# A new issue order for a gated long-convolution and mixer kernel: second-level table zeroed before the last level's index is made

## The chip, the cores and the metric

The kernel runs on one core of a Trainium2 chip. The core has TensorE (PE, matmuls), VectorE (DVE), ScalarE (ACT), GpSimd (POOL), and SyncE (SP), which here issues DMAs only. The metric is device microseconds of one execution. Before the change the median of three runs is 243.41 us (242.63 to 243.48).

## The reference: what is computed

```
x = A_q                                        # 2048 x 512, bf16
k_shift = sum over 4 taps of shifted A_k * A_shift_k
kv      = k_shift * A_v
y       = causal convolution of kv with A_ssm_k (length 2048, by FFT) + kv * A_ssm_D
h       = x + layernorm(x) * y
# mixer on layernorm(h)
g   = gelu(layernorm(.) @ w1); its four column quarters shifted by 1, -1, 2, -2 rows
x1  = . + g_shifted @ w2
out = h + x1 + gelu(layernorm(x1) @ w3) @ w4
```

## The kernel before

All data stays in SBUF. The program first records about 920 operations with what each reads and writes, and then emits them in a hand-over order, the text `ISSUE`: a list of operation numbers. Where an operation may run on either of two engines, a letter behind its number says which (`V` DVE, `A` ACT, `G` POOL). Each engine executes its own operations strictly in the order of that list and waits, where it must, for what an operation reads. So a late input holds back everything behind it on that engine. The microseconds given to `add` and its helpers are the cost model from which the list was searched; they are not executed.

The work runs in these steps. The names are those used below.

- **Loads.** SP issues `k0..k3`, `v0..v3` (L240, L244) and `h0..h3` (L249), each 512 KB, and eight transfers of q (L430), each 256 KB.
- **k side.** k is transposed on PE and copied (`kT`, L171 on ACT or L173 on DVE: all plain copies out of PSUM show one of these two lines). Four taps are PE matmuls (`psh`, L477). DVE multiplies by v (`kvq`, L481), for four row quarters and two column halves. SP moves each result into another layout by two SBUF-to-SBUF transfers, the k rows (`Rk`, L488).
- **h side.** POOL adds A_ssm_D into column 0 of h (L563, once for h0 and h2, once for h1 and h3); PE transposes (`pt`, L502), ACT or DVE copies (`Rh`).
- **First level.** PE matmuls `pah` (from `Rh`) and `pak` (from `Rk`, L518), 16 each, copied out as `Th` and `Tk` by ACT or DVE.
- **Second level.** 32 PE groups `pc` (L542 to L544) against the block-diagonal table `Wc`; each is copied out (`xt`). `Wc` is zeroed by 12 POOL memsets (L411) and then filled by four DMAs (L414).
- **Product.** Per pair of groups DVE does a complex product (`pr`, L674, and `Yr`, `Yi`, L688 and L690).
- **Inverse.** 16 PE groups `pg` (L744), copied out as `Gs`. When all 16 are done the PSUM pools are exchanged and the last level begins.
- **Last level.** 8 PE groups `py` (L797) against `Wf`, whose angles come from an index made by POOL (iota, L344) and two DVE passes each on two halves (`uf`, L351 and L354), and two ACT sines (L358). The result is scaled by the row's normalisation (`y`, L805 on ACT, L807 on DVE), gated with q (`hs`, L812), its statistics are taken (L620, L621), a Newton chain of ten small DVE operations (`rh`, L601 to L605 and others) gives the scale, and ACT or DVE normalises (`hn`, L840, L843). This is done in four blocks of four row tiles, b0 to b3.
- **Mixer.** For b0 and b1 PE transposes `hn`, for b2 and b3 SP does it by DMA transposes (L900). Then come the matmuls with w1 (L868, gelu on ACT, L872), w2 (L945, `x1` on DVE), w3 (L868) and w4 (L1014), and the stores.

q is normalised beside this: statistics (`bst`, L624), means, and a centring of each of 16 tiles (`qc`, L634 on ACT, L636 on DVE). ACT loads the gelu table (L423) once, after its last sine.

Of the kernel before, what the change touches and what calls it, by code (L numbers as in the profile page):

```python
# [42 lines left out]
19 89 91 4 87 78 1 0 2 30 92 31 22 5 20 33 88 23 7 6 8 25 12 32 24 34V 42 35 41 40 43 48 93 10 26 90 28 29 95 15  # L43
14 21 36 38 45 46 39 98 44 49 50 51 99V 100V 96A 104 9 54 139 47 18 105V 52V 55V 3 97A 56 37 17 53 57 11 101
102A 103A 107 106A 13 142 140 84 75 111 83 60 108 27 141V 143A 74 166 16 68 167A 112 144 113 115 116 114 160 76
80 230 228 229 231 63 240 241 253V 61 161A 79 158 254V 65 147 110 159A 145 148A 77 62 152 146V 119 153A 109 255A
151 120 156 157A 127 118 162 222 220 66 64 221 58 198 117 128 223 122 123 236 121 194 252A 124 237 246V 163A 131
59 199A 164 149 195A 247V 176 178 132 81 165A 172 177A 82 173A 179V 190 180 170 181A 191V 171A 245V 135 244A 168
192 224 227 136 67 182 174 193V 169A 183A 154 273 155V 175A 225 226 238 239 250V 275 69 188 189A 72 186 248V 184
187A 185A 70 272 71 73 281 283 282V 276 284A 285 138 277A 86 130 249V 251V 278 279A 280 295 196 296A 85 293 129  # L50
288 197A 290 287 286 125 307 234 294A 297 137 235 289A 291A 305 292 308A 300 302 134 233 232 126 306A 260 242
150 301A 298 133 210 216V 261 204 303A 211V 208 205A 200 209A 212 299 324 262 214 304 263 264 201A 243 274 213A
265 314 206 215V 202 315A 312 266 319 207A 203A 313A 317 327 309 320A 267 310 318A 311 332 328A 325 330 268 333A
217V 337 326A 269 259V 316 331A 270 218V 321 322 323 329 339 338A 381 334 335 340A 344 342 336 349 271 345A 341
# [74 lines left out]
def kernel(  # L133
# [927 lines left out]
```

## Time and profile before

| | us |
|---|---|
| profiled execution, its own time | 243.34 |
| its span | 241.5 |
| PE busy | 224.7 (93%) |
| DVE busy | 161.0 (67%) |
| ACT busy | 153.1 (63%) |
| POOL busy | 15.4 (6%) |

The profile gives times from the start of the span; 1.84 us of the execution lie outside it. PE's busy time holds matmuls on zeros (L440, L880) that only keep it running, so its 93% doesn't say that PE is the bound everywhere. The granted TensorE clock is full in all 40 slices. Rows of the timeline read: start, duration, engine, line, operation, and in brackets the idle time before it and what ended that. Rows with several pieces are merged.

### The profile page before, as it was taken

What the parts mean: (1) busy time and instruction counts of PE and PEld (TensorE: products, weight loads), DVE (VectorE), ACT (ScalarE), POOL (GpSimd) and SP (SyncE); (2) the same over time, 40 slices, a digit from 0 to 9 for tenths busy, and PEclk for the clock granted to TensorE, in tenths of its full rate; (3) what the DMA queues carried; (4) which work ended last, traced back from release to release, by engine and by line L of the source; (5) the groups of instructions that cost most, each with busy time, mean ns of one, the idle gap of its engine ahead of it and who ended that gap; (6) DMA issues with size and microseconds to landing.
All of it is one profiled execution on the core that took longest, in us unless ns stands there. A gap on an engine that the chain in (4) does not pass through costs nothing.

```text
span 241.5 us, 5031 instructions
## 1 busy us (share of the span) xinstructions
PE 224.7 (93%) x2069; PEld 147.6 (61%) x2069; DVE 161.0 (67%) x380; ACT 153.1 (63%) x205; POOL 15.4 (6%) x30
## 2 busy tenths in 40 slices
PE   8899987998899977999969999999999999999994
PEld 7899987897799864574434544444444444444454
DVE  6954999999999997999998899910440044004421
ACT  5788769999979998889657399763036204630000
POOL 2359300000000000000000000000000000000000
PEclk9999999999999999999999999999999999999999
DMA  6998876740000099100640025320002012001111
GB/s 218 391 374 203 168 187 213 174 91 3 0 3 0 20 343 390 39 0 0 88 84 5 1 53 99 61 52 3 10 22 54 0 24 65 0 0 42 46 43 45
DMA packets 22182, 21.82 MB, mean 90 GB/s; under 512 B 11916, under 2 KB 18704, under 8 KB 22160
## 3 DMA queue, kind: packets, MB, share of 16 engines
q1 hardware_dynamic: 21904, 21.37, 32.7%
q8 instruction: 16, 0.26, 0.5%
q10 hardware_dynamic: 256, 0.14, 0.2%
q14 instruction: 6, 0.05, 0.1%
HBM read 13.11 MB, written 2.10 MB: 63 GB/s over the span
## 4 chain that ended last, share of the span: by engine, by line
PE 51%; DVE 25%; DMA 12%; ACT 6%; issue 2%; SPq 1%; DVEq 0%; ACTq 0%
PE pw L868 23%; PE p L1014 20%; DVE kin L674 6%; DMA kin<-in_A_v_dram 5%; PE p L945 4%; DVE bst L620 4%; DVE ab L173 4%; ACT s L171 3%; DMA q_sb<-in_A_q_dram 3%; ACT ab L171 3%; DMA kin<-in_A_k_dram 2%; DVE ab L812 2%; DMA act<-ab 2%; DVE kin L688 1%; DVE bst L624 1%
## 5 line engine op out<-in xcount | busy, mean ns | idle before, releaser
L868 PE MATMUL pw<-act,wts 128*128 128x512 bf16 x288 | 64.0, 379 | 2.5 <-DMA act<-ab 1.9
L872 ACT ACTIVATE ab<-pw 128x512 bf16<-128x512 f32 x56 | 33.0, 596 | 38.4 <-PE pw L868 27.3
L1019 DVE TENSOR_TENSOR wts<-p,wts 128x1024 bf16<-128x1024 f32 (+2 forms) x10 | 10.1, 1012 | 62.0 <-PE p L1014 62.0
L868 PEld LDWEIGHTS <-wts 128*128 128x128 bf16 x288 | 28.0, 98 | 36.3 <-DMA act<-ab 2.4
L1014 PE MATMUL p<-wts,ab 128*128 128x512 bf16 (+1 forms) x238 | 48.9, 366 | 0.0
L1014 PEld LDWEIGHTS <-ab 128*128 128x128 bf16 x238 | 23.3, 98 | 25.3
L542 PE MATMUL pc<-ab,Wc 128*128 128x256 bf16 x128 | 30.7, 282 | 1.4 <-DVE ab L173 1.1
L171 ACT CAST s<-pc 128x1024 bf16<-128x1024 f32 x31 | 29.6, 1044 | 1.4 <-DVE kin L674 1.3
L544 PE MATMUL pc<-ab,Wc 128*128 128x128 bf16 x128 | 29.0, 227 | 0.0
L543 PE MATMUL pc<-ab,Wc 128*128 128x128 bf16 x128 | 28.0, 219 | 0.0
L543 PEld LDWEIGHTS <-Wc 128*128 128x128 bf16 x128 | 19.4, 151 | 1.4 <-issue 1.4
L674 DVE TENSOR_TENSOR kin<-s 128x2048 bf16<-128x2048 bf16 x16 | 19.4, 1221 | 0.6
L542 PEld LDWEIGHTS <-Wc 128*128 128x128 bf16 x128 | 19.4, 151 | 0.3
L544 PEld LDWEIGHTS <-Wc 128*128 128x128 bf16 x128 | 18.2, 142 | 0.0
L477 PE MATMUL psh<-ab 128*128 128x128 bf16 x256 | 15.6, 219 | 0.4 <-DVE kvq L481 0.4
L171 ACT CAST ab<-pah 128x1024 bf16<-128x1024 f32 x13 | 12.8, 1023 | 4.8 <-PE pah L518 4.8
L477 PEld LDWEIGHTS <-ab 128*128 128x128 bf16 x256 | 14.4, 98 | 0.9 <-issue 0.4
L945 PE MATMUL p<-wts,act 128*128 128x512 bf16 x64 | 15.0, 379 | 0.0
L481 DVE TENSOR_TENSOR kvq<-psh,kin 128x1024 bf16<-128x1024 f32 x8 | 9.7, 1218 | 4.8 <-DMA kin<-in_A_v_dram 4.8
L171 ACT CAST ab<-pak 128x1024 bf16<-128x1024 f32 x13 | 12.5, 1061 | 0.0
L951 DVE SCALAR_TENSOR_TENSOR s<-ab,rho,p 128x512 bf16<-128x512 bf16 x16 | 11.5, 739 | 1.2 <-PE p L945 1.1
L1000 DVE SCALAR_TENSOR_TENSOR wts<-s,mq,ab 128x512 f32<-128x512 bf16 x16 | 11.2, 749 | 0.2
(139 smaller groups left out, 316.3 us busy)
## 6 DMA issues: line engine op xcount, KB each, us to landing
wts<-in_B_w_dram SPq DMA_DIRECT2D x2, 1792.0 KB, 11.1
kin<-in_A_k_dram SPq DMA_DIRECT2D x4, 512.0 KB, 5.8
ab<-in_A_ssm_k_dram SPq DMA_DIRECT2D x4, 512.0 KB, 8.6
kin<-in_A_v_dram SPq DMA_DIRECT2D x4, 512.0 KB, 13.6
q_sb<-in_A_q_dram SPq DMA_DIRECT2D x8, 256.0 KB, 6.1
kin<-kvq SPq DMA_DIRECT2D x16, 128.0 KB, 5.1
out_dram<-wts SPq DMA_DIRECT2D x14, 128.0 KB, 2.3
Wc<-ab SPq DMA_DIRECT2D x4, 384.0 KB, 5.3
```

The source lines that it names most:

```text
L171: A.copy(o, src)
L477: T_.matmul(pv[:, g, i, :], lhsT=row(g, 4 * qr + i - j), rhs=dg()[:, 2 * g + cc, j, :], start=(j == 0), stop=(j == 3))
L542: T_.matmul(pv[:, kk], lhsT=W[0], rhs=T[:, :, 2 * k1:2 * k1 + 2, :], start=True, stop=False)
L543: T_.matmul(pv[:, kk, :, 0, :], lhsT=W[1], rhs=T[:, :, 2 * k1 + 1, :], start=False, stop=False)
L544: T_.matmul(pv[:, kk, :, 1, :], lhsT=W[2], rhs=T[:, :, 2 * k1, :], start=False, stop=True)
L674: v(1.13, lambda: V.tensor_tensor(out=prs(), in0=xs(0).unsqueeze(1).to_broadcast([P, 2, 2, 512]), in1=xs(1).unsqueeze(2).to_broadcast([P, ...
L868: T_.matmul(ps[:], lhsT=wt(w)[:, k, m * P:(m + 1) * P], rhs=xT()[:, k, 4 * b * P:(4 * b + 4) * P], start=(k == 0), stop=(k == DC - 1))
L872: add({"A": 0.49}, lambda: A.activation(dst(), X[pkey][:], ACT.Gelu_apprx_tanh), r + [pkey, "gelu"], [key])
L945: T_.matmul(ps[:, i, :], lhsT=gT()[:, m, t + i + 2 + off[m], :], rhs=wt("w2")[:, m, :], start=(m == 0), stop=(m == 3))
L951: v(0.66, lambda t=t, i=i, key=key: V.scalar_tensor_tensor(out=qn()[:, t + i, :], in0=hn()[:, t + i, :], scalar=rho[:, t + i:t + i + 1], i ...
L1000: v(0.66, lambda j=j, i=i, t=t + i: V.scalar_tensor_tensor(out=ofb()[:, j, i], in0=qn()[:, t, :], scalar=mq[:, t:t + 1], in1=hs()[:, t, :] ...
L1014: T_.matmul(ps[:, i, x0:x1], lhsT=g2(b % 2)[:, m, s0:s0 + P], rhs=wt("w4")[:, m, x0:x1], start=(m == 0), stop=(m == FC - 1))
```

## The change

**Zeroing first.** POOL's queue, after the small gate operation, was: iota and hand-over for `uf`, the h addition, the 12 memsets with the second h addition after two of them. The 12 memsets now wait only for the gate, and the `uf` iotas wait for the memsets; the operation `gt2` that ordered the two goes. The POOL order is now: 3 memsets, h addition (h0, h2), 8 memsets, h addition (h1, h3), 1 memset, then for each half of `uf` an iota and the first of its two passes. Those two first passes have moved from DVE to POOL by their letter.

**k rows.** The transfers may be issued from SP or from ACT's queue, by a letter `S` or `A`.

**Scaling.** The two scalings of a `py` group become one operation with two instructions, on one engine.

**Cost model.** Some of its figures change (0.6 to 0.615, 0.08 to 0.14 and so on); these aren't executed.

**Orders.** `ISSUE` is replaced as a whole. In it all sixteen k rows have the letter `S`.

The order of SP, first part, before:

```
k3 k0 k2 k1 h2 h0 v0 h3 h1 v1 v2 q q v3 | Rk1 x2, q q, Rk0 x2, Rk2 x2, Rk3 x2 | q q, Wc x4 | second half's Rk, with q q among them
```

and after:

```
k2 k1 k0 k3 h0 v1 h2 v2 v0 h3 v3 h1 q q q q | Rk0 x2, Rk2 x2, Rk1 x2, Rk3 x2 | Wc Wc q Wc Wc q | second half's Rk | q q
```

ACT, from its last `kT` to the first `Tk`, before and after:

```
Wf Rh Wf Th7 gelu-table Th4 Th3 Rh Th0 qc Th2 qc Th5 Th15 Th13 Th6 | Tk4 ...
Th1 Th5 Th4 Rh10 Th3 Rh11 Th2 Wf Th0 Th10 Th13 | Tk2 ...
```

From there to ACT's last `Gs`, before: 13 Tk, 4 Th, 31 xt, 10 Gs, 1 qc. After: 12 Tk, 4 Th, 29 xt, 13 Gs, 2 qc, 1 Wf, the gelu table.

DVE, from its last `kT` to the first `Tk`, before and after:

```
uf x4, kvq0 Rh kvq1 kvq2, bst x4, 2 mq, 2 qc, Rh, kvq3, bst x3, kvq1', bst, mq, kvq0', mq, 2 qc, kvq2' | Tk5 ...
kvq1 kvq2 Rh Rh kvq3 Th6 kvq0, bst x4, 2 mq, 3 qc, uf, qc, bst x2, kvq0', bst, kvq2', Th7 | Tk1 ...
```

From there to DVE's last `Gs`, before: 3 Tk, 3 Th, 1 xt, 6 Gs, 1 kvq, 8 bst, 6 qc. After: 4 Tk, 2 Th, 3 xt, 3 Gs, 2 kvq, 9 bst, 3 qc, 1 uf. The 32 product operations and four copies of Wf are in both. After its last `Gs` DVE does 1 qc, the new one 5 qc and the end of q's Newton chain.

PE, after the four `kT` transposes, before: `psh0, pt, pt, psh1, pah7, psh2, pah4, pah3, pt, pt, pah0, psh3, pah2 ...`; after: `psh1, psh2, pt, pt, psh3, pah1, pah6, psh0, pah4, pah5, pt, pah3, pt, pah2, psh0', psh2', pah0, pah10, pah7, pah13, pak1, pak2 ...`.

Last level on DVE, before: one `y` half, hs0, 2 bst, hs1, 2 bst, then b0's Newton chain, within which hs2, hs3 and the statistics of b1 stand. After: one whole `y`, hs0, hs1, hs2, hs3 and all eight statistics of b0 and b1, with the Newton chains of b0 and b1 alternating at their end; b3 then goes ahead of b2. `hn`: 8 on ACT and 8 on DVE before, 10 and 6 after. On PE the order is, before: w1 for b0 and b1, two w2 pairs, w1 for b2, a w2 pair, w1 for b3; after: w1 for b0 and b1, two w2 pairs, w1 for b3, w1 for b2. SP's DMA transposes go xT 8, 11, 10, 9, 15, 14, 12, 13 before and 14, 12, 13, 15, 8, 11, 10, 9 after.

```diff
-            i = int(word.rstrip("AVG"))
+            i = int(word.rstrip("AVGS"))
...
-    for hf in range(2):
-        iota(1.05, lambda hf=hf: uf(hf), [[1, 16], [32, 64]], 16 * hf, ("uf", hf), ["C", "gate"])
-        phase(0.68, lambda hf=hf: uf(hf), k1F, offF, ("uf", hf), ["C"])
-    gt2 = cst.tile([P, 2], I32)
-    add({"G": 0.2}, lambda: G.tensor_copy(gt2[:], ...
     for q in range(4):
         for a in range(3):
             add({"G": 0.95}, lambda q=q, a=a: G.memset(
-                X["Wc"][:, q, a].rearrange("p d n k -> p (d n k)").bitcast(U32), 0), ["W", "gate2"], [("wz", q, a)])
+                X["Wc"][:, q, a].rearrange("p d n k -> p (d n k)").bitcast(U32), 0), ["W", "gate"], [("wz", q, a)])
...
+    for hf in range(2):
+        iota(1.05, lambda hf=hf: uf(hf), [[1, 16], [32, 64]], 16 * hf, ("uf", hf),
+             ["C"] + [("wz", q, a) for q in range(4) for a in range(3)])
+        phase(0.68, lambda hf=hf: uf(hf), k1F, offF, ("uf", hf), ["C"])
...
-            dma(0.63, lambda g=g: nc.sync.dma_start(
+            add({"S": 0.63, "A": 0.5}, lambda e, g=g: (nc.scalar if e == "A" else nc.sync).dma_start(
...
-        for i in range(2):
-            def scaled(e, i=i, t=2 * u + i):
+        def scaled(e):
+            for i in range(2):
+                t = 2 * u + i
...
-            add({"A": 0.53, "V": 0.6}, scaled, ["W", key, ("rq", 0)], [("y", u % 4, i)])
+        add({"A": 1.18, "V": 1.22}, scaled, ["W", key, ("rq", 0)], [("y", u % 4)])
```

More of the change, by code (lines that the diff above doesn't have):

```diff
@@ L402 @@
     hold()
-    for hf in range(2):
-        iota(1.05, lambda hf=hf: uf(hf), [[1, 16], [32, 64]], 16 * hf, ("uf", hf), ["C", "gate"])
-        phase(0.68, lambda hf=hf: uf(hf), k1F, offF, ("uf", hf), ["C"])
-    gt2 = cst.tile([P, 2], I32)
-    add({"G": 0.2}, lambda: G.tensor_copy(gt2[:], X["kin"][:, 20480:24576].rearrange(
-        "p (a x) -> p a x", a=2)[:, :, 0:2].bitcast(I32).rearrange("p a x -> p (a x)")), [("uf", 0), ("uf", 1), "C"], ["gate2"])
     for q in range(4):
@@ L588, in turned @@
                     V.tensor_scalar(o, x, -1.0, None, op0=MUL)
[L590 removed]
+            add({"V": 0.45, "A": 0.95}, turned, [("Wf", 0, hf)], [("Wf", 1, hf, c), ("kvq", 0), ("kvq", 1)], lock=True)
     mvq = cst.tile([P, NT, 2], F32)
@@ L636, in centre @@
                 V.tensor_scalar(X["q_sb"][:, t, :], X["q_sb"][:, t, :], mq[:, t:t + 1], None, op0=ADD)
-        add({"A": 0.71, "V": 0.325}, centre, [("mq", t // 4), ("bst", t)], [("qc", t)])
+        add({"A": 0.69, "V": 0.27}, centre, [("mq", t // 4), ("bst", t)], [("qc", t)])
     def rsqrt_q():
@@ L1001 @@
                     out=ofb()[:, j, i], in0=qn()[:, t, :], scalar=mq[:, t:t + 1], in1=hs()[:, t, :], op0=SUB, op1=ADD),
-                  ["W", "HH"] + [("y", k, l) for k in range(4) for l in range(2)] + [("x1", t + i), ("hs", t // 2)],
+                  ["W", "HH"] + [("y", k) for k in range(4)] + [("x1", t + i), ("hs", t // 2)],
                   [("of", j, i)])
```

84 lines of the change are left out of this document (41 added, 43 removed), and 7 rows, old and new, of the table ISSUE.

## The prediction

> **What bounds the kernel now.** I first cut the span into stretches, to see which engine is full where. After the time range, the columns are its length, the busy time (and instructions) of PE, weight loads, DVE, ACT and POOL, the granted clock, the DMA share and GB/s.
>
> ```profile
> 0.00:36.40 36.40, 33.36 (x557) 31.47 (x558) 27.26 (x61) 26.48 (x32) 15.38 (x30) 1.00 0.86 257
> 36.40:93.00 56.60, 49.91 (x716) 46.94 (x715) 55.48 (x81) 54.92 (x61) 0.00 (x0) 1.00 0.37 105
> 93.00:109.00 16.00, 14.19 (x163) 9.21 (x164) 14.14 (x51) 13.38 (x22) 0.00 (x0) 1.00 0.27 106
> 109.00:122.70 13.70, 11.56 (x64) 5.40 (x63) 13.22 (x53) 10.21 (x16) 0.00 (x0) 1.00 0.36 49
> 122.70:241.50 118.80, 115.73 (x570) 54.61 (x570) 50.86 (x139) 48.07 (x79) 0.00 (x0) 1.00 0.17 35
> ```
>
> From 36.4 to 93.0 us DVE idles 1.12 us and ACT 1.68: both are the bound, and only these gaps could be won. From 122.7 PE is full. Before 36.4, DVE and ACT have time to spare, 9.1 and 9.9 us. So the question is what work is left when the full stretch begins, and how the last level hands over to the matmuls. The chain of work that ended last names that hand-over (first line), and the timeline has its steps:
>
> ```profile
> 118.45 4.22 DMA act<-ab
> ...
> 94.28 0.69 ACT L805 ACTIVATE wts<-py,rq 128x512 bf16<-128x512 f32 x1 [0.64 <-PE py L797]
> 95.00 0.75 DVE L807 TENSOR_SCALAR wts<-py,rq 128x512 bf16<-128x512 f32 x1 [1.62 <-ACT wts L805]
> 95.78 0.69 DVE L812 TENSOR_TENSOR ab<-wts,q_sb 128x1024 bf16<-128x1024 bf16 x1
> 104.06 0.16 DVE L827 SCALAR_TENSOR_TENSOR nb<-mvh,rh 128x4 f32<-128x4 f32 x1
> 108.99 1.02 PE L868 MATMUL pw<-act,wts 128*128 128x512 bf16 x4 [0.34 <-ACT act L171]
> 117.22 3.62 PE L945 MATMUL p<-wts,act 128*128 128x512 bf16 x16
> 122.71 3.63 PE L868 MATMUL pw<-act,wts 128*128 128x512 bf16 x16 [1.88 <-DMA act<-ab]
> ```
>
> The last copies before the pool exchange end at 93.0 (the bound of the second stretch); hs0 starts at 95.78, b0's scale is ready at 104.2, PE starts w1 at 108.99, and it stalls 1.88 us for b2's DMA transposes.
>
> The front is set by the loads: SP's issues, and the moments at which PE, POOL and DVE stop waiting for a load:
>
> ```profile
> 11.99 0.34 SPq L244 DMA_DIRECT2D kin<-in_A_v_dram  x1
> 20.89 1.27 SPq L488 DMA_DIRECT2D kin<-kvq  x2
> 23.49 7.49 SPq L488 DMA_DIRECT2D kin<-kvq  x6
> 9.49 1.07 PE L452 MATMUL pk<-ident,kin 128*128 128x128 bf16 x16 [0.24 <-DMA kin<-in_A_k_dram]
> 12.12 0.31 POOL L563 TENSOR_TENSOR ab<-ab,dcol 128x2 bf16<-128x2 bf16 x1 [1.94 <-DMA ab<-in_A_ssm_k_dram]
> 14.51 1.23 DVE L481 TENSOR_TENSOR kvq<-psh,kin 128x1024 bf16<-128x1024 f32 x1 [1.53 <-DMA kin<-in_A_v_dram]
> 17.10 0.20 POOL L563 TENSOR_TENSOR ab<-ab,dcol 128x2 bf16<-128x2 bf16 x1 [2.10 <-DMA ab<-in_A_ssm_k_dram]
> 19.63 1.23 DVE L481 TENSOR_TENSOR kvq<-psh,kin 128x1024 bf16<-128x1024 f32 x1 [2.30 <-DMA kin<-in_A_v_dram]
> 21.83 1.22 DVE L481 TENSOR_TENSOR kvq<-psh,kin 128x1024 bf16<-128x1024 f32 x1 [0.97 <-DMA kin<-in_A_v_dram]
> DMA to landing us min/median/max: 13.2/13.6/14.6
> 35.28 0.69 PE L518 MATMUL pak<-WA,kin 64*128 64x128 bf16 x16
> 36.40 3.88 ACT L171 CAST ab<-pak 128x1024 bf16<-128x1024 f32 x4
> ```
>
> The landing line is that of the v loads. By SP's order these are the landings of loads 4, 6, 7, 9, 10 and 11: 9.5, 12.1, 14.5, 17.1, 19.6 and 21.8. v3, issued at 11.99, lands 14.6 later, at 26.6. The last k row is issued at 30.4 (23.49 + 7.49, less its own 0.6), and the first `pak` runs at 35.28, 4.9 later.
>
> **The change, part by part.** *Front.* Landings go by place in the queue, so the new order gives v1 (6th) 12.1, h2 (7th) 14.5, v2 about 15.8, v0 (9th) 17.1, h3 19.6, v3 (11th) 21.8 and h1 (12th) about 24.2, one more step of 2.4. v3 gains 4.8 us. But kvq0, whose k rows now stand first on SP, has become DVE's last: kvq3 to 23.0, Th6 to 24.1, kvq0 to 25.3 (about 1.15 each; the 1.23 of the rows overlaps). Eight k rows at 0.63 follow, the last issued at 29.7 and landed at 34.6: against 35.28, 0.7 is gained at most. But `pak` stands behind other PE work, and ACT isn't ready for it:
>
> ```profile
> L358 ACT ACTIVATE Wf<-kin,mpi 128x1024 bf16<-128x1024 int32 x2 | 2.3, 1174 | 0.0
> L171 ACT COPY s<-pt 128x2048 bf16<-128x2048 bf16 x2 | 3.7, 1870 | 0.6 <-PE pt L502 0.6
> L423 ACT ACT_TABLE_LOAD x1 | 1.3, 1283 | 0.0
> L423 ACT ACTIVATE warm<-warm 128x1 f32<-128x1 f32 x1 | 0.2, 203 | 0.0
> L634 ACT ACTIVATE q_sb<-q_sb,mq 128x512 bf16<-128x512 bf16 x2 | 1.4, 723 | 0.3 <-DVE mq L629 0.3
> L624 DVE BATCH_NORM_STATS2 bst<-q_sb 128x6 f32<-128x512 bf16 x6 | 3.9, 683 | 0.0
> 16.00 1.96 PE L477 MATMUL psh<-ab 128*128 128x128 bf16 x32
> ```
>
> h1 at 24.2, POOL's addition 0.2, 32 transposes 1.9 (like 32 matmuls of `psh`): Rh10 starts at 26.3. Two Rh, five Th (3.88 / 4 = 0.97 each) and a sine, 3.7 + 4.8 + 1.2 = 9.7, bring ACT's first `Tk` to 36.0. DVE holds it a little longer: pah13 needs the PSUM buffer that kvq2' frees, and from q's landing, about 26.6, DVE does 7 `bst`, 4 `qc`, a `uf` pass, means and two kvq, 8.7 us, to 35.3; then pah13, Th13, `Tk`: 36.6. Before 36.40: +0.2.
>
> *The full stretch.* From the first `Tk` to the last `Gs`, ACT has 58 copies in both kernels (13+4+31+10 and 12+4+29+13). The new list adds a sine, the table load with its activation, and a `qc`: 1.17 + 1.28 + 0.20 + 0.72 = 3.4 us. The old order had done these in the front, where ACT waited for data; the new ACT idles there, from its last `kT` (about 11) until h2 (14.5), two `pt` and psh3 (5.8) and pah1 let it do Th1, at about 20.8. With the same 1.7 us of gaps ACT ends 3.6 later, at 96.6. DVE's list is even: one copy fewer (-1.15), a kvq (+1.15), a `bst` (+0.6) and a `uf` pass (+0.6) more, three `qc` fewer (-0.9). It can't take over what ACT is late with, as the letters are fixed; it fills the wait with five `qc`.
>
> *hs0.* Before, 2.8 after the last `Gs`. Now py0 is ready 1.28 after it (94.28) and two scalings at 0.7 follow on DVE: 2.7, so -0.1.
>
> *To the first w1.* hs0 to b0's scale took 8.4. The new list has in between 4 hs (0.6 each), 8 statistics (0.6), 8 aggregations (0.1) and about 16 Newton steps (2.0 together): 10.1, +1.7. Then ACT does two hn, a copy, hn, a copy, 3 x 0.72 + 2 x 0.97 = 4.1, where 4.8 passed before: -0.7. Together +1.0.
>
> *The stall.* PE wants b2's w1 after the scale by 4.1, then 8.2 (108.99 to 117.22), 3.5 for w2 and 3.5 for b3: 19.3. On ACT, hn12 ends after six hn, four copies, four gelus and itself, 10.8; then SP issues seven transposes:
>
> ```profile
> L900 SPq DMA_TRANSPOSE act<-ab x8: 1188/1232/1296, 114.5 to 125.1; - x8
> DMA to landing us min/median/max: 2.4/2.5/4.2
> L872 ACT ACTIVATE ab<-pw 128x512 bf16<-128x512 f32 x56 | 33.0, 596 | 38.4 <-PE pw L868 27.3
> ```
>
> Six at 1.23 and the last one's landing, 2.5, are 9.9: b2 is there at 20.7, a stall of 1.4 for 1.9, -0.5.
>
> *POOL.* Memsets, additions and iotas keep their price. The two first `uf` passes leave DVE, 1.55 us by their row, but from a place after which DVE waited 1.53 for v: nothing won. Their price on POOL isn't in the trace; the nearest rows:
>
> ```profile
> 9.90 1.55 DVE L351 TENSOR_SCALAR kin<-kin,pf 128x1024 int32<-128x1024 int32 x2
> L411 POOL MEMSET Wc<- 128x1024 uint32 x12 | 10.9, 959 | 0.0
> L344 POOL IOTA kin<- 128x1024 int32 x2 | 2.0, 1036 | 0.0
> masks.py:199 POOL TENSOR_SCALAR_AFFINE_SELECT ident<-ident 128x128 bf16<-128x128 bf16 x1 | 0.3, 292 | 0.1
> ```
>
> From 0.8 (DVE's own) to eight times the 128-column select, 2.3; I take 1.04, the iota's, of the same size and type. The last memset ends at 25.3, the iota at 26.3, the pass at 27.4, and DVE asks at about 30.4: hidden up to 4.1 us a pass. By the Trainium skill, GPSIMD Engine Reference, section "Elementwise — side-by-side cycle accounting", a tight loop takes at best about 1.8 cycles per element; at its 1.2 GHz that is an estimate of 1.5 us for 1024, and the sum would be the same. `Wc` is zeroed at 25.3, before SP asks for it behind the k rows, at 30.3.
>
> *The rest.* All sixteen k rows have the letter S: nothing goes to a second queue, 0. `gt2` was POOL time nobody waited for, 0. From b2's w1 on PE has the same matmuls, and I find no late input in the new order: 0.
>
> Sum: 0.2 + 3.4 - 0.1 + 1.0 - 0.5 = +4.0 on the profiled 243.34: 247.3. The median of the runs is 0.07 above that execution, so 247.3 stands for both. About 0.5% (1.2 us) is what a measurement can tell from no change.
>
> **Rivals.** *A, not slower: the loads drain evenly.* Loads 4 to 6 land 1.3 us apart, later ones 2.4. If the new order kept 1.3, v3 lands at 18.6 and h1 at 19.9. Then PE's order is the limit: from the fourth `kT` transpose at 10.5, four psh and two `pt` at 1.9 and two pah bring psh0 to 22.6, kvq0 to 23.8, the last k row to 33.1 and ACT's first `Tk` to 33.9, 2.7 sooner: 244.6. If the 1.7 us of ACT's gaps and the +1.0 close with it, 241.9. It decides from h1 before 21 on. The row at 17.10, for the ninth load, speaks against it. By the Trainium skill, DMA: Bandwidth & Descriptors, section "Specifications", the ceiling is 435 GB/s; twelve loads of 512 KB would take an estimated 14.5 us. The trace, with its ninth at 17.1, disagrees.
>
> *B, slower still: POOL is slow.* At 6 us a pass DVE stands 2 us at its `uf` step, with kvq0' and all behind it: 249.3. It decides at 4.1; no row is near that.
>
> *C: b0's later scale doesn't cost.* DVE is busy 14.14 of 16.0 and 13.22 of 13.7 us there; if its whole list, with two hn fewer, and not b0's scale paces PE, the +1.0 goes: 246.3, still slower.
>
> **How the numbers follow.** Forecast 0.44 and C 0.22, slower but for 0.02; A 0.27, about half of it faster and half no change, by how many gaps close with it; B 0.07. So faster 0.14, same 0.15, slower 0.71. The range reaches down to A with its gaps closed in part, 242.6, and up to B or h1 one 2.4 step later, 249.5.
>
> **What the new profile would show.** ACT nearly idle from 11 to 20; POOL's second h addition near 24; the first `Tk` copy on ACT near 36.6; the table load inside the full stretch; the last `Gs` on ACT near 96.6, hs0 near 99.3, w1 near 113.5; a wait for DMA transposes near 1.4. I am wrong if the h addition comes before 21, if ACT reaches `Tk` before 34, or if PE has a stall after its first w1 that the old order hadn't.

## The result, and the profile after

The changed kernel takes 246.79 us in the median (245.90 to 247.12), the kernel before 243.32 (242.63 to 243.48), four runs each. The recorded ratio is 1.0135, with a 95% interval of 1.0109 to 1.0161; the quotient of the two medians, 1.0143, lies within it. The prediction was 247.3 and slower, with a range of 242.6 to 249.5. The profiled execution took 247.04, with a span of 245.3 against 241.5.

Below are the stretches of the prediction's first table, with the same columns. The first three cuts are at the same events (first `Tk` copy on ACT, last `Gs` copy on ACT, first w1). The last cut is at the second of the two w1 blocks whose input comes through DMA transposes, where that table had the first of them; both are b2's. The last line is one single microsecond out of the second stretch.

```profile
0.00:36.87 36.87, 32.92 (x529) 31.22 (x530) 28.07 (x58) 20.77 (x25) 17.82 (x31) 1.00 0.82 256
36.87:95.56 58.69, 52.93 (x749) 50.33 (x746) 56.42 (x84) 57.45 (x65) 0.00 (x0) 0.97 0.39 108
95.56:112.22 16.66, 14.52 (x166) 9.16 (x166) 16.17 (x56) 13.79 (x22) 0.00 (x0) 1.00 0.19 74
112.22:130.07 17.85, 15.12 (x79) 6.94 (x81) 16.13 (x75) 12.75 (x21) 0.00 (x0) 1.00 0.35 60
130.07:245.30 115.23, 111.51 (x540) 52.78 (x550) 47.30 (x113) 44.25 (x72) 0.00 (x0) 1.00 0.16 33
...
39.00:40.00 1.00, 1.00 (x14) 0.82 (x13) 1.00 (x2) 1.00 (x2) 0.00 (x0) 0.50 1.12 358
```

In the second stretch ACT is now full: 1.24 us idle of 58.69, where it had 1.68 of 56.60. DVE has 2.27 idle. And the granted clock, full throughout before, is 0.50 at 39 to 40 us; it is so from 37.9 to 41.3. The steps, from the timeline of the changed kernel:

```profile
24.31 0.20 POOL L562 TENSOR_TENSOR ab<-ab,dcol 128x2 bf16<-128x2 bf16 x1 [3.17 <-DMA ab<-in_A_ssm_k_dram]
24.38 1.23 DVE L480 TENSOR_TENSOR kvq<-psh,kin 128x1024 bf16<-128x1024 f32 x1 [0.18 <-PE psh L476]
25.63 6.13 SPq L487 DMA_DIRECT2D kin<-kvq  x8
26.49 1.20 POOL L351 TENSOR_SCALAR kin<-kin,pf 128x1024 int32<-128x1024 int32 x1
36.87 3.77 ACT L171 CAST ab<-pak 128x1024 bf16<-128x1024 f32 x4
40.48 1.19 ACT L358 ACTIVATE Wf<-kin,mpi 128x1024 bf16<-128x1024 int32 x1
42.72 1.01 ACT L171 CAST ab<-pak 128x1024 bf16<-128x1024 f32 x1 [1.05 <-PE pak L517]
44.36 1.28 ACT L422 ACT_TABLE_LOAD   x1
88.73 0.68 DVE L687 TENSOR_TENSOR kin<-kin 128x1024 bf16<-128x1024 bf16 x1
85.28 10.28 ACT L171 CAST ab<-pg 128x1024 bf16<-128x1024 f32 x11
97.99 0.69 DVE L814 TENSOR_TENSOR ab<-wts,q_sb 128x1024 bf16<-128x1024 bf16 x1
103.33 4.83 ACT L806 ACTIVATE wts<-py,rq 128x512 bf16<-128x512 f32 x8 [0.96 <-DVE mvh L620]
107.40 0.16 DVE L829 SCALAR_TENSOR_TENSOR nb<-mvh,rh 128x4 f32<-128x4 f32 x1
108.05 1.51 ACT L842 ACTIVATE ab<-ab,nb,rh 128x512 bf16<-128x512 bf16 x2
112.22 1.02 PE L870 MATMUL pw<-act,wts 128*128 128x512 bf16 x3 [1.10 <-ACT act L171]
124.65 3.63 PE L870 MATMUL pw<-act,wts 128*128 128x512 bf16 x16 [0.22 <-DMA act<-ab]
130.07 3.61 PE L870 MATMUL pw<-act,wts 128*128 128x512 bf16 x16 [1.79 <-DMA act<-ab]
```

The second h addition on POOL is at 24.31, where the prediction had 24.2; kvq0 ends at 25.6 (25.3), and the last of the eight k rows is issued at about 31.0 (25.63 + 7/8 of 6.13; 29.7). Both Wf sines come late, one of them and the table load inside the full stretch, as the prediction's list had it. The row at 42.72 is new: ACT waits 1.05 us for a `pak` that stands on TensorE behind matmuls run at half the clock (32 of `psh` take 2.84 us from 39.44, and 1.96 from 42.87). In the last level b0's scale is ready 9.6 us behind hs0 (107.40 + 0.16, against 97.99), but ACT is still busy with its last eight `y` and starts b0's `hn` behind them, at 108.05, without a wait. Then w1 starts at 112.22. PE now stalls 0.22 ahead of b3's w1 and 1.79 ahead of b2's.

The chain that ended last, from the page of the changed kernel, has ACT at 14% of the span, where it had 6% before, and DVE at 14% instead of 25%:

```profile
PE 55%; ACT 14%; DVE 14%; DMA 11%; issue 3%; SPq 1%; DVEq 0%; ACTq 0%
```

To set the two traces side by side three rows of the kernel before are still missing: its last product on DVE, b0's first `hn` on ACT (which there waited for DVE's scale), and the second of its transposed w1 blocks:

```profile
86.77 0.69 DVE L690 TENSOR_TENSOR kin<-kin 128x1024 bf16<-128x1024 bf16 x1
104.26 1.52 ACT L840 ACTIVATE ab<-ab,nb,rh 128x512 bf16<-128x512 bf16 x2 [0.74 <-DVE nb L827]
128.13 3.62 PE L868 MATMUL pw<-act,wts 128*128 128x512 bf16 x16
```

| from, to | predicted | before | after | measured |
|---|---|---|---|---|
| start, first `Tk` on ACT | +0.2 | 36.40 | 36.87 | +0.5 |
| first `Tk`, end of the last product on DVE | | 51.06 | 52.54 | +1.5 |
| last product, end of the last `Gs` on ACT | +3.4 for both | 5.55 | 6.15 | +0.6 |
| last `Gs`, hs0 | -0.1 | 2.77 | 2.43 | -0.3 |
| hs0, first w1 | +1.0 | 13.21 | 14.23 | +1.0 |
| first w1, second transposed w1 | -0.5 | 17.33 | 17.85 | +0.5 |
| from there to the end | 0 | 115.18 | 115.23 | 0 |
| sum | +4.0 | 241.5 | 245.3 | +3.8 |

(At its second transposed w1 the kernel before had done one w2 pair more, 3.62 / 2 = 1.81; that is moved from the sixth step, 19.14, to the last, 113.37.)

So the sum came out right, but two of its terms did not: the full stretch cost 2.1 instead of 3.4, the stall grew instead of shrinking. And half of the 2.1 seems to come from a clock that no term knew of.

### The profile page after: what moved, and what is told of

The parts are those of the page before. It is cut to its first block, busy times and chain, and to the rows that moved or that the text cites. A ratio compares the mean times of both kernels' runs of the same rounds, so it can differ in the third digit from the quotient of the medians.

```text
span 245.3 us, 5014 instructions
## 1 busy us (share of the span) xinstructions
PE 227.0 (93%) x2057; PEld 150.4 (61%) x2069; DVE 164.1 (67%) x382; ACT 149.0 (61%) x201; POOL 17.8 (7%) x31
## 4 chain that ended last, share of the span: by engine, by line
PE 55%; ACT 14%; DVE 14%; DMA 11%; issue 3%; SPq 1%; DVEq 0%; ACTq 0%
PE pw L870 22%; PE p L1016 20%; ACT ab L171 8%; ACT s L171 6%; DMA q_sb<-in_A_q_dram 5%; PE p L947 4%; DVE bst L619 4%; DMA kin<-in_A_v_dram 4%; PE pc L541 2%; DMA act<-ab 2%; DVE ab L814 2%; PE psh L476 2%; DVE bst L623 2%; PE pc L543 1%; PE pc L542 1%
## 5 line engine op out<-in xcount | busy, mean ns | idle before, releaser
L1021 DVE TENSOR_TENSOR wts<-p,wts 128x1024 bf16<-128x1024 f32 (+2 forms) x10 | 10.1, 1012 | 60.4 <-PE p L1016 57.1
L1016 PEld LDWEIGHTS <-ab 128*128 128x128 bf16 x238 | 23.3, 98 | 25.3
L171 ACT CAST s<-pc 128x1024 bf16<-128x1024 f32 x29 | 28.6, 1133 | 0.2 <-PE pc L543 0.2
L171 ACT CAST ab<-pah 128x1024 bf16<-128x1024 f32 x12 | 12.1, 1028 | 10.2 <-PE pah L517 10.2
L476 PE MATMUL psh<-ab 128*128 128x128 bf16 x256 | 16.2, 226 | 0.0
L476 PEld LDWEIGHTS <-ab 128*128 128x128 bf16 x256 | 15.2, 102 | 0.4 <-issue 0.2
L874 ACT ACTIVATE act<-pw 128x512 bf16<-128x512 f32 x16 | 9.0, 611 | 7.0 <-PE pw L870 6.8
L171 ACT CAST ab<-pak 128x1024 bf16<-128x1024 f32 x12 | 12.0, 1134 | 1.0 <-PE pak L517 1.0
L171 ACT CAST ab<-pg 128x1024 bf16<-128x1024 f32 x13 | 12.4, 1148 | 0.0
## 6 DMA issues: line engine op xcount, KB each, us to landing
q_sb<-in_A_q_dram SPq DMA_DIRECT2D x8, 256.0 KB, 10.1
```

What stands on the lines that cost most here:

```text
L171: A.copy(o, src)
L476: T_.matmul(pv[:, g, i, :], lhsT=row(g, 4 * qr + i - j), rhs=dg()[:, 2 * g + cc, j, :], start=(j == 0), stop=(j == 3))
L874: add({"A": 0.49}, lambda: A.activation(dst(), X[pkey][:], ACT.Gelu_apprx_tanh), r + [pkey, "gelu"], [key])
L1016: T_.matmul(ps[:, i, x0:x1], lhsT=g2(b % 2)[:, m, s0:s0 + P], rhs=wt("w4")[:, m, x0:x1], start=(m == 0), stop=(m == FC - 1))
L1021: v(0.58 * (hi - lo) * (x1 - x0) / D, lambda j=j, lo=lo, hi=hi, x0=x0, x1=x1, key=key: V.tensor_tensor(out=obb()[:, j, lo:hi, x0:x1], in0= ...
```

## The experiments

Each ran beside the kernel before on the same chip; the chips differ a little (medians of the kernel before 242.86, 243.41 and 243.22 in the three groups), so ratios are compared. Stretches come from one profiled execution each.

### Halves: the old last level, the old front

The orders of the two kernels are cut at the pool exchange and joined crosswise. The edit of one, in words (the other is its mirror image; the runs are called by their first two characters):

```diff
 x2_old_tail
 new orders up to the last Gs
-new orders from y on, y in one operation of two instructions
+old orders from y on, y in two operations
```

> The changed kernel up to the last Gs eviction, and from y on the orders of the kernel before, with y scaled in two instructions of one tile each as there. Theory (from hs on the new order costs 1.6 us: b0's scale comes 1.1 us later behind hs0 and the wait for the transposes ahead of b2's w1 doesn't shrink): 244.9 to 245.7. Rival (the path from hs0 to the end is equal and all of the loss lies ahead of hs0): 246.4 to 247.1.

> The converse: the kernel before up to the last Gs eviction, and from y on the changed kernel's order and its y scaled two tiles at a time. Theory: 1.6 us above the kernel before, 244.6 to 245.4. Rival (the tail is equal): 243.0 to 243.7. If the two parts add up, this one's loss and the loss of the changed kernel's front with the old tail make 3.5 us together.

x2 took 244.38, ratio 1.0060 (1.0033 to 1.0088); x3 took 244.70, ratio 1.0068 (1.0042 to 1.0095). Both theories held within about half a microsecond: the new last level costs about 1.6 us, the new front about 1.5, together 3.1 of the 3.3 that the whole change costs by its ratio. The full stretch in the window view, first of x2 (new front), then of x3 (old front):

```profile
35.27:92.95 57.68, 51.59 (x750) 49.26 (x746) 56.25 (x84) 57.49 (x65) 0.00 (x0) 1.00 0.41 109
```

```profile
37.19:93.81 56.62, 49.98 (x716) 46.96 (x715) 55.49 (x81) 54.91 (x61) 0.00 (x0) 1.00 0.39 111
```

The old front's stretch is 56.62 again, as in the kernel before (56.61). The new front's is 57.68, with the clock at 1.00 throughout: 1.1 more, not 2.1 and not 3.4. x2's twelve runs also show the clock: six with a mean of 0.993 or less have a median of 245.2 us, six at 0.998 or more one of 243.9. So the 1.5 us of the new front are a mean over both kinds.

### The clock

```diff
 def stage_a(w, i, ring):
+    for _ in range(4 if key in (("pah", 7), ("pah", 13), ("pak", 1), ("pak", 2), ("pak", 6)) else 0):
+        T_.matmul(ps[:, 0:P], lhsT=zero[:, 0:P], rhs=zero[:, 0:P], start=True, stop=True)
     for ee in range(4):
```

> The changed kernel with four more matmuls of zeros (128 rows, 128 columns, about 0.24 us in all) at the head of five of TensorE's operations between 33 and 38 us (pah7, pah13, pak1, pak2, pak6), each into the operation's own tile, which the real matmuls then overwrite. Theory (the granted clock falls to 0.50 for 3.4 us at 38 because TensorE ran half-row matmuls with gaps just before, and that costs about 1 us): the clock stays at 1.00 through 36 to 43, and the time falls by 0.5 to 1.0, to 245.8 to 246.3. Rival 1 (the fall of the clock is hidden under ACT): same, 246.5 to 247.1. Rival 2 (the zeros lie on the path of the pak evictions): 247.0 to 248.0. Rival 3: the clock falls all the same.

x4 took 245.41, ratio 1.0088 (1.0057 to 1.0120), and the clock was 0.999 to 1.000 in all six runs. The theory holds. By the ratios the gain is (1.0135 - 1.0088) x 243 = 1.1 us, a little over the range of 0.5 to 1.0, and the intervals just overlap. But that isn't the clock alone: only two of the changed kernel's four runs had the fall (a mean of 0.993), and x4's profiled execution is also 0.8 shorter in the sixth step of the table (17.0 for 17.85, see "The last level"). The price is better read from the stretch:

```profile
36.89:94.51 57.62, 51.69 (x756) 49.43 (x755) 56.05 (x84) 57.44 (x64) 0.00 (x0) 1.00 0.38 102
```

57.62, as in x2, so the fall of the clock is what made 58.69 of it; 1.05 of that is ACT's wait at 42.72. By the Trainium skill, TensorE: Matmul & The Clock Gate, section "What's actually happening", the array goes to half its clock after an idle window of about 3.4 us and back to full after a busy one as long, and the window runs freely, so that the moment of a change varies from run to run. The trace agrees on the length (0.50 from 37.9 to 41.3). The clock entries kept with the traces fit a window that runs on: full clock lasts 27.3 us before the fall in the changed kernel, 13.7 in y1, 30.7 in y4 and 17.1 before the first fall in z2 (kernels below), which is 8, 4, 9 and 5 times 3.41. The trace differs in one thing: TensorE was not idle before the fall. In the 3.4 us ahead of it TensorE was busy for 2.1, with 64-row matmuls and waits, and ahead of y1's fall for 2.9; yet in the kernel before the clock stayed up although it was busy for only 1.8 of the 3.4 us from 84.1 on, with matmuls of 128 rows and columns. So the share of busy time alone doesn't decide, and what does isn't shown here.

The zeros are no sure remedy. y3 and z3, which keep x4's front, had one run of twelve with 0.993, against eight of sixteen in the changed kernel and x2. With another front or start around the zeros there were more: one of twelve in y2, three of six in y1 and in y4, five of twelve in z4. In the profiled execution of y1 the fall lies at 17.9 to 21.3, far ahead of the zeros; in that of y4 it lies at 36.1 to 39.5, among them.

### What sets the full stretch

The first of three kernels (x1) undoes the zeroing-first part alone and puts ACT's sines and table load back into its free time:

```diff
         iota(1.05, lambda hf=hf: uf(hf), [[1, 16], [32, 64]], 16 * hf, ("uf", hf),
-             ["C"] + [("wz", q, a) for q in range(4) for a in range(3)])
+             ["C", "gate"])
 POOL: gate, uf0, uf0', uf1, h, uf1', 9 memsets, h, 3 memsets
 DVE:  kvq1, uf0'', kvq2, uf1'' ...
 ACT:  last kT, Wf, Wf, gelu table, Th1 ...
```

> The changed kernel with the zeroing-first part alone undone: the second-level index rows are made ahead of the zeroing again, both in time for ACT's free stretch before its first Th eviction, and the two Wf sines and the gelu table load (3.7 us in the profile of the changed kernel) go back there on ACT. The k rows (all on SP, as in the changed kernel), the loads' order and everything from h on stay those of the changed kernel. Theory (the zeroing-first part pushes ACT's work into its full stretch): the last Gs eviction comes 2 to 3 us earlier than 95.4 and the time falls from 246.8 to 244.0 to 244.8. Rival 1 (ACT isn't what sets the last Gs; DVE's and PE's order of the new search do): 246.3 to 247. Rival 2 (POOL's earlier passes cost DVE or the h additions as much): 246 to 248.

It took 253.82, ratio 1.0451 (1.0406 to 1.0495): none of the three, with the first `Tk` at 47.12. In the timelines of POOL and DVE of this run:

```profile
15.13 8.09 POOL L403 MEMSET Wc<- 128x1024 uint32 x9
15.67 8.09 DVE L352 TENSOR_SCALAR kin<-kin 128x1024 int32<-128x1024 int32 x1
24.81 3.37 DVE L352 TENSOR_SCALAR kin<-kin 128x1024 int32<-128x1024 int32 x1
24.91 2.73 POOL L403 MEMSET Wc<- 128x1024 uint32 x3
```

DVE's second pass over an index half, 0.69 us in the kernel before, takes 8.09 us, and ends half a microsecond behind the last of nine memsets that POOL runs meanwhile (15.13 + 8.09 = 23.22, against 23.76). The second half's pass does the same with three memsets: 3.37 us. So the pass hardly moves while memsets run. It fits this that the kernel before held the memsets back with `gt2`, and that the new one holds the index back until all twelve are done. By the Trainium skill, SBUF — State Buffer, section "SBUF: two separate sides", DVE and GpSimd share a port pair which an instruction takes whole, the other waiting. The trace agrees, and adds that DVE got little or no turn between two memsets: the pass ends 0.54 us behind the last one, and alone it takes 0.69.

So the second kernel makes the index first and keeps the fence, on top of x4:

```diff
-        memsets wait for "gate"; iotas wait for all memsets
+        iotas wait for "gate"; gt2 waits for both uf; memsets wait for gt2
 DVE:  kT, uf0', uf0'', kvq1, uf1', uf1'', kvq2 ...
 ACT:  last kT, Wf, Wf, gelu table, Th1 ...
```

> x4_warm_pe with the zeroing-first part undone in full: the index is made ahead of the zeroing and the small gt2 operation holds the memsets back until DVE's four passes are done, as in the kernel before; the two Wf sines and the gelu table load go into ACT's free stretch before Th1. So it is x1_sines_early with the memsets kept off DVE's index passes. Theory 1 (x1's 8.1 us index pass on DVE came from POOL's memsets running beside it): the four passes take 0.7 to 0.8 us each again. Theory 2 (what zeroing first cost was ACT's 3.6 us of sines and table load in the full stretch): with ACT relieved of these, the last Gs on ACT comes 1.0 to 2.4 us earlier than the 94.5 of x4_warm_pe (no more, because DVE's own list then sets the end), ratio 0.999 to 1.005. Rival to theory 2 (DVE and the hand-over between the engines set the last Gs anyway): ratio 1.006 to 1.011.

It took 244.50, ratio 1.0056 (1.0028 to 1.0084). Theory 1 holds: the same passes take 0.69 again (first two rows below; then two of TensorE's operations in the full stretch). For theory 2 the ratio lies between the two ranges, and the stretch decides: it didn't shrink (57.59, where x4 had 57.62), so the theory falls. x1, which also has the sines and the table load in the front, shows the same: 57.62 (47.12 to 104.74).

```profile
13.36 0.69 DVE L352 TENSOR_SCALAR kin<-kin 128x1024 int32<-128x1024 int32 x1
15.94 0.69 DVE L352 TENSOR_SCALAR kin<-kin 128x1024 int32<-128x1024 int32 x1
40.07 1.96 PE L475 MATMUL psh<-ab 128*128 128x128 bf16 x32
42.63 1.96 PE L475 MATMUL psh<-ab 128*128 128x128 bf16 x32
```

```profile
37.73:95.32 57.59, 51.70 (x756) 49.43 (x754) 55.59 (x83) 55.05 (x61) 0.00 (x0) 1.00 0.38 106
```

ACT has 2.4 us less to do than in x4 (55.05 busy, not 57.44), and the stretch is 57.59 as before. The waits of ACT in it, in total, times and longest:

```profile
ACT ab L169 <- PE pak L519: 1.4, 2, 1.0
ACT ab L169 <- PE pah L519: 0.9, 1, 0.9
ACT s L169 <- PE pc L545: 0.7, 1, 0.7
```

What ACT no longer does there it waits: for `pak` and `pah` behind TensorE's two `psh` of the second half at 40.07 and 42.63, 1.96 us each, and then for the first `pc`. (In the kernel before only one `psh` lies in the stretch, at 38.50; the one before it runs at 33.12.) In the new order the late sine and table load lie beside these. The better ratio against x4 (by 0.8 us, the intervals overlap) isn't explained by the stretch.

The converse, in the old order:

```diff
 ACT, kernel before:
-    ... Rh, Wf, Wf ... gelu table ... qc ... | Tk4 Tk2 Tk6 Tk1 qc Tk0 Tk7 Tk3, Th10 ...
+    ... Rh, Wf ...                       | Tk4 Tk2 Tk6 Tk1 qc Tk0 Tk7 Tk3, Wf, gelu table, qc, Th10 ...
```

> The kernel before with nothing changed but ACT's order: the second Wf sine, the gelu table load with its activation, and one qc move from ACT's free time in the front to behind Tk3, inside the full stretch (1.2 + 1.3 + 0.2 + 0.7 = 3.4 us, the same work that the new order has there). Theory of the prediction (ACT's list sets the last Gs; what is added to it comes out at the end, less ACT's own gaps of 1.7): 1.7 to 3.4 us slower, ratio 1.007 to 1.014. Rival (DVE's list sets the last product and with it the last Gs; in y2_index_first the stretch stayed at 57.6 us though ACT had 2.4 us less to do): ratio 0.999 to 1.004, with the last product on DVE 51.1 to 51.5 us behind the first Tk copy, as in the profile of the kernel before (51.1).

It took 247.80, ratio 1.0198 (1.0172 to 1.0224), more than either theory. The stretch and two of its waits:

```profile
37.46:97.80 60.34, 51.35 (x716) 47.97 (x715) 54.98 (x80) 58.16 (x65) 0.00 (x0) 0.97 0.35 97
```

```profile
DVE kin L673 <- ACT s L170: 4.1, 2, 3.5
PE pc L541 <- ACT ab L170: 2.5, 1, 2.5
```

60.34 instead of 56.6: here the 3.4 us cost 3.7, with a fall of the clock among them. TensorE waits 2.5 for the last `Th` behind the table load, and DVE then 4.1 for the first products' inputs; in TensorE's wait the clock falls too (0.50 from 48.1 to 51.6), and its mean is 0.984 to 0.993 in the six runs. A first fall, from 24.3 to 27.7, lies ahead of the work that was moved, and the first `Tk` comes at 37.46, 1.1 later than in the kernel before; with the 3.7 that makes the 4.8 by which the span is longer (246.3 for 241.5). So the mechanism of the prediction is real, but it depends on the place: at this place in the old order nothing else holds TensorE and DVE, in the new order TensorE's `psh` do. That it is these `psh` is read from the rows; no run moved them.

### The start of TensorE

On DVE the new order has `pf` ahead of the clearing of the zero tile, so TensorE's first matmuls run at 2.42 us instead of 1.20.

```diff
 DVE: 
-    pf, warm (with zero), uW, kz ...
+    warm (with zero), kz, pf, uW ...
 PE, on top of x4: one more group of zeros ahead of the k transposes
```

> The changed kernel with the extra zero matmuls of x4_warm_pe (it ran at 1.0088 of the kernel before, with the clock full from 36 to 43), and with the start of the kernel before: DVE clears the tile of zeros ahead of pf again, so that TensorE's first matmuls run at 1.2 us instead of 2.4, and one more group of eight zero matmuls stands among them (moved from the full stretch). Theory (the new order starts TensorE's zero matmuls later, so TensorE stays at half its rate, 12 matmuls in 1 us instead of 22, until 6.8 to 10.3 us where the kernel before left that by 5, and the whole front moves by that): 0.3 to 1.0 us less than x4_warm_pe, a ratio of 1.005 to 1.008, with the second psh done 0.3 to 1.4 earlier than 16.2. Rival (the front is set by the loads, not by TensorE's rate at the start): the ratio stays at 1.008 to 1.010.

It took 245.73, ratio 1.0105 (1.0069 to 1.0140): no gain, as the rival has it. But three of its six runs had the fall of the clock; the other three have a median of 244.94, against 245.94, so a small gain at full clock isn't excluded. DVE's second product with v:

```profile
16.82 1.22 DVE L478 TENSOR_TENSOR kvq<-psh,kin 128x1024 bf16<-128x1024 f32 x1 [2.65 <-DMA kin<-in_A_v_dram]
```

The first comes as early as in x4 (12.94 and 12.95), but this next one waits 2.65 us for v: here the load is the limit. In seven profiled executions of the new front (y3 and y4, below, stand apart) the first `Tk` follows the second h addition on POOL at a nearly fixed distance: 22.55 and 35.27 in x2, 24.31 and 36.87 in the changed kernel (12.6 and 12.7 later); with the zeros of x4, 23.44 and 36.89, 23.39 and 36.58 (z4), 23.48 and 36.94 (z3), 24.56 and 37.73 (y2), 25.24 and 38.77 (y1), so 13.2 to 13.5. The twelfth load lands at 22.6 to 25.2, differently in each execution, and that moves everything behind it.

### The second queue

```diff
-    Rk(1, g1), Rk(2, g1), Rk(3, g1), Rk(0, g1): S
+    Rk(1, g1), Rk(2, g1), Rk(3, g1), Rk(0, g1): A
```

> x4_warm_pe with the part of the change that the new order leaves unused: four of the first eight k rows get the letter A and are issued from ACT's queue, two ahead of Th1, one behind Th4, one behind the first Rh copy on ACT. Theory (the first pak waits for other work on PE and ACT, not for the k rows): no gain; ratio 1.008 to 1.013, the upper end where ACT stands waiting for kvq3 or kvq0. Rival (two queues land the k rows earlier and pak with them): ratio 1.002 to 1.007, with the first Tk before 36.

It took 246.49, ratio 1.0137 (1.0103 to 1.0172): no gain, rather a loss. Its transfers (KB each, median us from issue to landing):

```profile
kin<-kvq SPq DMA_DIRECT2D x12, 128.0 KB, 4.0
kin<-kvq ACTq DMA_DIRECT2D x4, 128.0 KB, 9.2
```

Two rows issued by ACT at 14.1 and 17.1 stand beside the big loads and land 9.2 and 9.4 us later. The third, issued at 24.9, takes 4.2, and the row that SP issues at the same time 5.3: it is the moment that makes the difference, not the queue. What comes late is `pak`, and ACT waits for it:

```profile
38.53 1.01 ACT L169 CAST ab<-pak 128x1024 bf16<-128x1024 f32 x1 [1.27 <-PE pak L518]
```

No transfer holds `pak`: TensorE goes from the `pah` ahead of it to `pak` without a wait. In this execution the clock falls to 0.50 at 36.1, under the first `pak` and its zeros. Three of the six runs have such a mean (0.991 to 0.993); the other three have a median of 246.21, 1.0115 of the kernel before, still above x4's 1.0088. What makes up that rest isn't shown.

### The last level

> x4_warm_pe with one thing moved in the last level on DVE: b0's Newton chain starts right behind b0's own statistics, with hs2, hs3 and b1's statistics within and behind it, as in the kernel before. y in two scalings, hn, the blocks' order and the transposes stay. Theory (b0's scale stands behind work of b1 and this delays the first w1 by 1.0): w1 comes 13.2 us behind hs0 instead of 14.2, the time falls by 0.6 to 1.0, ratio 1.0045 to 1.0065. Rival (b0's scale doesn't pace PE; DVE's whole list does, and b1 or the transposes become late instead): ratio 1.008 to 1.010, with a new wait on PE ahead of b1's, b3's or b2's w1.

```diff
 DVE, on top of x4, from hs0 on:
-    ... hs1, 2 stats, hs2, hs3, then b0's chain between b1's statistics
+    ... hs1, 2 stats, b0's chain, with hs2, hs3 and b1's statistics between its steps
```

y3 took 246.02, ratio 1.0111 (1.0079 to 1.0143): no gain. hs0, ACT's last y, b0's scale, and the first w1:

```profile
97.61 0.69 DVE L815 TENSOR_TENSOR ab<-wts,q_sb 128x1024 bf16<-128x1024 bf16 x1
103.46 4.83 ACT L807 ACTIVATE wts<-py,rq 128x512 bf16<-128x512 f32 x8 [1.47 <-DVE nwt L603]
106.42 0.15 DVE L830 SCALAR_TENSOR_TENSOR nb<-mvh,rh 128x4 f32<-128x4 f32 x1
112.34 1.02 PE L871 MATMUL pw<-act,wts 128*128 128x512 bf16 x3 [1.10 <-ACT act L169]
```

b0's scale comes 8.8 behind hs0 (start to start), 0.6 sooner than in the changed kernel. But hs2 and hs3 now come later, and the buffers that they free are awaited by ACT's last eight y, which start at 103.46 and end at 108.3; b0's `hn` stands behind them on ACT, so w1 is 14.7 behind hs0, 0.5 later than before the edit. ACT's list is thus a second chain, and the later one: in x4 too ACT's last `y` end at 107.1, 0.6 behind b0's scale. The next edit was meant to shorten that one instead:

```diff
-        y of a py group: one operation, both instructions on one engine
+        y of a py group: two operations; first pair: tile 0 on DVE, tile 1 on ACT
 PE:  py0, py1, then zeros (py1 stood behind twelve zeros)
```

> x4_warm_pe with the scaling of y split again, one tile per operation, and the first pair shared: DVE scales its first tile, ACT its second ahead of its last two qc, and TensorE does py1 right behind py0 instead of behind twelve zero matmuls. All other orders of the last level stay new. Theory (the last level's 1.0 us ahead of the first w1 comes from ACT: with the whole first pair on DVE, ACT starts on y 2.8 us behind the last Gs instead of 1.3, and all its y stand ahead of b0's hn): hs0 comes 0.5 to 0.7 earlier behind the last Gs (1.8 instead of 2.4) and w1 13.2 to 14.2 behind hs0, so that the last Gs to w1 takes 15.2 to 16.1 us instead of 16.7; the time falls by 0.5 to 1.4 against x4_warm_pe, ratio 1.003 to 1.007. Rival (what is gained ahead of w1 is lost to the DMA transposes): w1 comes earlier by as much, the wait ahead of b2's w1 grows by it, ratio 1.008 to 1.011.

z3 took 245.39, ratio 1.0110 (1.0080 to 1.0140): no gain either. DVE's first y, and hs0:

```profile
96.31 0.75 DVE L809 TENSOR_SCALAR wts<-py,rq 128x512 bf16<-128x512 f32 x1 [1.19 <-ACT wts L807]
97.09 0.69 DVE L814 TENSOR_TENSOR ab<-wts,q_sb 128x1024 bf16<-128x1024 bf16 x1
```

DVE waits 1.19 us for ACT's y of the same group before it does its own, so that sharing the pair brings nothing: hs0 is 2.6 behind the last `Gs` (94.53), w1 14.24 behind hs0 (111.33). ACT's last eight `y` still start 5.3 behind hs0 (102.44), as in x4 (102.28), so ACT's chain wasn't shortened. Only DVE's was shortened alone, in y3. x2 shows that the whole old order brings 13.2 back; that both chains must be shorter for that is read from the rows.

The stall is left. In x4, y1 to y4 and z3, which have the new last level, TensorE waits 1.29 to 1.32 us ahead of b2's w1, as the prediction had it (1.4), and the sixth step of the table is 17.0. In the changed kernel, in x3 and in x1 it is 17.8, and there the issues of the transposes show one outlier (shortest, median, longest, in ns):

```profile
L902 SPq DMA_TRANSPOSE act<-ab x8: 1189/1217/2072, 116.5 to 127.5; - x8
```

From the first issue to the start of the last it is 11.0 us here and in x3, 10.9 in x1, and 9.9 to 10.1 in the other six. One issue of 2.0 to 2.1 us instead of 1.2, the fourth of eight in all three, fits the difference. It isn't shown to be the cause: y2, y4 and z3 have one of 1.9 to 2.1 too, but it is the first of the eight and did no harm. The three with the long fourth issue are also the three without x4's zeros. What makes an issue long wasn't tried.

### Parts undone together

```diff
 y2_index_first
-new orders from y on
+old orders from y on, y in two operations
 start of TensorE as in y1_warm_start
```

> What is left when the parts that cost are undone together: y2_index_first with the kernel before's order and scaling from y on (as in x2_old_tail) and with TensorE's zero matmuls started early (as in y1_warm_start). The new orders of the loads, of k, h, and of the two middle levels stay. If the parts add up: 1.0056 (y2) less 0.0068 (the new tail, by x3) and up to 0.003 for the start, ratio 0.996 to 1.001, a version that may beat both. Rival (the new front costs 1 us through its own loads: the twelfth lands at 22.6 to 25.2 and the first Tk follows 13 later): ratio 1.001 to 1.006.

z4 took 243.57, ratio 1.0023 (1.0000 to 1.0046). That is 0.001 above the range of the sum and in that of the rival; the interval reaches both. Five of its twelve runs had the fall of the clock, with a median of 244.25; the other seven have 243.21, the same as the kernel before (243.22). So the parts add up where the clock stays full, and what stays is the new order of loads, k, h and the middle levels, which at best equals the old one. Its w1 (110.00) follows hs0 (96.80) by 13.2, as in the kernel before.

No version that was run beats the kernel before.

## Why the prediction was right, and where it was not

- **Front, +0.2.** Right. h1 at 24.2 was 24.31, the first `Tk` at 36.6 was 36.87. The distance between them, 12.4 in the prediction, is 12.6. That the times themselves meet so closely is in part luck: the landing varies by 2.7 us between executions (22.6 to 25.2), which the prediction's range had only as one step later.
- **POOL.** The pass takes 1.20 and 1.31 us, not 1.04; both are below the other estimate, of 1.5. It is hidden as said. But POOL's pass doesn't seem to be free for DVE. In the changed kernel three `qc` on DVE beside the second one take 1.75 us, where four take 1.13 once POOL is idle:

```profile
28.73 1.75 DVE L635 TENSOR_SCALAR q_sb<-q_sb,mq 128x512 bf16<-128x512 bf16 x3
94.26 1.13 DVE L635 TENSOR_SCALAR q_sb<-q_sb,mq 128x512 bf16<-128x512 bf16 x4
```

- **The full stretch, +3.4: the step that failed.** "With the same 1.7 us of gaps ACT ends 3.6 later" was wrong. Without the fall of the clock the stretch grows by 1.0 to 1.1 (x1, x2, x4, y1, y2, y3, z3, z4). ACT's list is busy 2.5 longer (57.44 against 54.93; its 58 copies take 0.9 less than I had), and 1.5 of that went into its gaps, 1.68 before and 0.18 in x4. y2 and x1 show that even without this work the stretch is as long. What does make it longer: 0.4 up to the last product on DVE, and 0.6 behind it, where ACT copies some seven `Gs` and DVE three, instead of six and five. That is from the rows; a better split wasn't tried.
- **The clock, not in the sum: +1.1 in the profiled execution.** The term above was 1.3 too high even with it, 2.4 without. The stall (1.0 too low) and the first `Tk` (0.3 too low) made up the rest: the total was right by errors that cancel.
- **hs0, -0.1, and the first w1, +1.0.** Right in size (-0.3, +1.0). For the second the reason was another: b0's scale is ready 9.6 behind hs0, not 10.1, and w1 follows it by 4.7, not 4.1. These are two errors that cancel. What ends 10.2 behind hs0 is ACT's last `y` (103.33 + 4.83 = 108.16), a chain that the prediction didn't follow; y3 shows that an earlier scale alone doesn't bring w1 forward.
- **The stall, -0.5.** Nearly right in six profiled executions (17.0 for 17.33: -0.3), and +0.5 in the one shown, which fits one slow issue.
- **k rows.** Nothing went to the second queue, and 0 was right. In y4, which uses it, there is no gain.
- **Rivals.** A (even landings) is out: 24.3 and not 19.9. B (POOL at 6 us a pass) is out: 1.3. C (the later scale doesn't cost) is out as put: w1 and with it the end come 1.0 later, and x3 loses 1.6 by the last level alone.
- **Signs of being wrong.** Two of the three stayed away (24.31 for the h addition, 36.87 for `Tk`). The third came, by 0.22 us: the stall ahead of b3's w1, which the old order hadn't. x3 and x1 have it too (0.22 and 0.11); x4, y1 to y4 and z3 don't, so it goes with the slow issue.

## What to carry to other kernels

Work that was moved onto a full engine cost its whole length in one place (z2) and nothing in another, where that engine would have waited anyway (y2). So before such a term is added up, look at what the engine waits for at that place in the new order, and charge only what is longer than that wait. A single resummed total can be right by errors that cancel, so compare a prediction with the result step by step, at the same events. And when TensorE has thin places, a fall of the clock is a term of its own, with a chance and a price (here 8 of 16 runs of the new front without the zeros, and about 1 us).

## What the runs showed of the hardware that was not expected

- A DVE pass over 1024 int32 per partition, 0.69 us alone, took 8.09 us while POOL ran nine memsets of 0.9 us back to back, and 3.37 us beside three.
- The granted clock fell to 0.50 for 3.4 us behind 3.4 us in which TensorE was busy for 2.1, mostly with 64-row matmuls; with zero matmuls of 128 rows among them it stayed up in six runs of six, in other orders not always. Full clock before a fall lasted a whole number of times 3.41 us (8, 4, 9 and 5 in four executions).
- At the start TensorE runs at half its rate (11 to 13 matmuls of 128 columns in 1 us, against 22 later) while the window view shows a clock of 1.00; the clock entries kept with the trace begin only at 10.6 us in the changed kernel, at 6.3 in x4 and at 4.4 in the kernel before. In the changed kernel 48 k transposes took 3.61 us; in x4 they took 2.85:

```profile
9.00 3.61 PE L451 MATMUL pk<-ident,kin 128*128 128x128 bf16 x48
```

- A k row issued by ACT beside the loads took 9.2 us to land; one issued by ACT later took 4.2, and one by SP at that time 5.3.
